# Loads one batch ahead, stores from the ScalarE queue, 128-partition q/k and two-bank PSUM tiles in a fused attention and gated FFN kernel

## The chip, the cores and the metric

The kernel runs on one core of a Trainium2 chip. The metric is the device time of one execution in microseconds (us); runs of one kernel in this study lie within some 1 to 3% of each other. A profile's span is about 1.7 us shorter than the time quoted for the same run. A run over 1.5% above the fastest of its kernel is counted as slow; only fast runs enter the ratios.

Engines: PE is TensorE, PEld its weight loads, DVE is VectorE, ACT is ScalarE, POOL is GpSimd, SP is SyncE, which here only issues transfers. The traces list each one's instructions in an order of their own, called its queue here (in the page of the kernel before, 2211 of PE and 269 of DVE).

## The reference, cut to what matters

```python
def _attn_ref(q, k, v):                 # (4, 8, 768, 64) each
    block, window = (32, 16)
    k_sum = k.reshape(B, H, nb, block, D).max(axis=3)     # 24 summary keys
    v_sum = v.reshape(B, H, nb, block, D).mean(axis=3)
    # scores on a band |i-j| < 16, and on the 24 summaries (+ log 32); one softmax
    # over both; the result times [v, v_sum]
def _moe_ref(x, w_gate, w_val, w_out):  # x: 3072 tokens x 512, d_ff 1536
    gate = 1 / (1 + exp(-(x @ w_gate)))
    return (gate * (x @ w_val)) @ w_out
```

## The kernel before

Queries go in 12 tiles of 64 per head; each tile sees 96 keys and 24 summaries. The kernel emits small units: T (transpose q and k of a head pair, build windows and summaries), S (scores and exp), V (sum v over blocks and spread the sums to all 12 tiles), A (attention times v), X (transpose the result into the FFN's input). Batch 0 goes through them alone, the head. After that the units of batch b+1 are strewn among the matmuls of the FFN of batch b. FFN of batch 3 runs alone.

```python
psum = ctx.enter_context(tc.tile_pool(name="psum", bufs=8, ...))   # one bank each, for all
...
def load_qk(b, p):       # 96 partitions of 8 tokens
    st = stg_pool.tile([128, 1024], FP32, ...)
    nc.sync.dma_start(out=st[0:96]..., in_=tap[b, 2*p:2*p+2].rearrange("h (p t) d -> p h (t d)", t=8))
...
def u_T(p):              # pk and pq are two tiles
    pk = ps([128, 8, 96], BF16, "pk")       # 8 transposes; VectorE copies and reduces it
    pq = ps([128, 8, 96], BF16, "pq")       # 8 transposes
    nc.scalar.copy(out=qT..., in_=view(pq, 0, [[1, 96], [96, 8]]))
...
def u_V():
    ...                  # 12 matmuls into vsp
    nc.vector.tensor_copy(out=vx[96:120, 0, :, 0:64], in_=vsp[96:120]...)
    nc.vector.tensor_copy(out=vx[96:120, 1:NQ, :, 0:64],
                          in_=vx[96:120, 0:1, :, 0:64].to_broadcast([NS, NQ - 1, H, 64]))
...
def u_2(hf, tt, part):   # second FFN layer; when a tile is done:
    nc.scalar.mul(out=ot, in_=m3, mul=0.5)
    nc.sync.dma_start(out=out[r:r + 128, :], in_=ot)      # same queue as the loads
...
for b in range(B):       # loads and casts of batch b+1 are emitted here, at the start of FFN b
```

The softmax here doesn't subtract the row's maximum and nothing guards it: scores larger than these inputs give would overflow.

## Time and profile before

313.96 us (313.77 to 314.0, 3 runs). To compare kernels I cut each profile at the second gate activation (the head and the first two FFN units are done) and at the last output tile of each batch. The lines that carry the reading stand in the prediction, whose own cuts lie up to 1.5 us earlier.

| us | head | FFN 0 + att. 1 | FFN 1 + att. 2 | FFN 2 + att. 3 | FFN 3 | end | span |
|---|---|---|---|---|---|---|---|
| before | 48.3 | 71.7 | 70.9 | 71.6 | 46.7 | 3.1 | 312.3 |

FFN 3 shows what a batch's FFN costs when nothing disturbs it. The other stages are some 25 us longer, and attention of a batch is 11.2 us of pure TensorE work: the rest is waiting, half clock (groups of four matmuls that take about 1.3 us instead of 0.65, at a granted clock of 0.50 from 76 to 81 us) and switching.

### The profile page before, as it was taken

The numbers are of one execution on the slowest core, as the hardware profiler recorded it, in microseconds if no ns is written. First come the engines' busy times: TensorE is split into PE (matmuls) and PEld (weight loads), VectorE is DVE, ScalarE is ACT, GpSimd is POOL, SyncE is SP. The second block draws the span as 40 slices with busy tenths as digits, with TensorE's granted clock in tenths as the row PEclk, the third lists the DMA queues.
The fourth block names the chain that finished last, engine by engine and source line by source line (L and its number), as shares of the span: only waits on it lengthen the run. The fifth ranks groups of instructions, "written<-read, shape, count | busy, mean of one in ns | idle before, by whom it ended". The sixth has DMA issues, their size and how long they took to land.

```text
span 312.3 us, 5516 instructions
## 1 busy us (share of the span) xinstructions
PE 261.3 (84%) x2211; PEld 145.6 (47%) x2224; DVE 159.1 (51%) x269; ACT 115.3 (37%) x221; POOL 83.6 (27%) x112
## 2 busy tenths in 40 slices
PE   1384669993995996899799997798799999999995
PEld 0332536661542543564455443563365545666542
DVE  5545944469836642685775311684676311444200
ACT  2640623341530553263165322362164333333221
POOL 8475863049700000675000000675000000000000
PEclk9999859997897999599999999799799999999999
DMA  7999999619600115995000025995000112000022
GB/s 216 263 214 320 385 292 252 239 41 241 151 36 0 60 43 176 280 197 115 0 3 2 34 93 182 262 212 121 2 0 2 37 67 101 2 0 3 0 101 101
DMA packets 54713, 37.84 MB, mean 121 GB/s; under 512 B 37792, under 2 KB 43936, under 8 KB 54688
## 3 DMA queue, kind: packets, MB, share of 16 engines
q1 hardware_dynamic: 54688, 37.49, 44.0%
q8 instruction: 17, 0.28, 0.4%
q14 instruction: 8, 0.07, 0.1%
HBM read 31.20 MB, written 6.29 MB: 120 GB/s over the span
## 4 chain that ended last, share of the span: by engine, by line
PE 62%; DMA 16%; DVE 12%; POOL 4%; SPq 3%; issue 1%; ACT 1%; POOLq 0%; ACTq 0%; DVEq 0%
PE m L326 21%; PE gp L309 17%; PE vp L309 16%; DMA qst<-in_q_dram 8%; DMA vst<-in_v_dram 7%; DVE vx L251 4%; PE av L262 3%; POOL vx L149 3%; SPq L109 2%; DVE kTx L204 2%; DVE xs L270 2%; PE br L283 2%; PE vsp L243 1%; PE sc L224 1%; DVE P L233 1%
## 5 line engine op out<-in xcount | busy, mean ns | idle before, releaser
L315 DVE SCALAR_TENSOR_TENSOR hT<-gate,vp 128x384 bf16<-128x384 f32 x96 | 52.8, 552 | 73.2 <-PE vp L309 73.0
L309 PE MATMUL gp<-xT,wg 128*128 128x384 bf16 x384 | 83.1, 341 | 0.0
L309 PE MATMUL vp<-xT,wv 128*128 128x384 bf16 x384 | 81.7, 337 | 0.0
L314 ACT ACTIVATE gate<-gp 128x384 f32<-128x384 f32 x96 | 47.2, 492 | 67.5 <-DVE hT L315 34.1
L326 PE MATMUL m<-wo,hT 128*128 128x512 bf16 x275 | 66.3, 384 | 0.8 <-issue 0.2
L309 PEld LDWEIGHTS <-wv 128*128 128x128 bf16 x384 | 38.7, 101 | 27.4 <-issue 4.0
L309 PEld LDWEIGHTS <-wg 128*128 128x128 bf16 x384 | 35.5, 101 | 24.0 <-issue 4.2
L124 POOL CAST qkbf<-kst 96x1024 bf16<-96x1024 f32 x12 | 12.8, 1067 | 108.9 <-DMA kst<-in_k_dram 90.4
L326 PEld LDWEIGHTS <-hT 128*128 128x128 bf16 x288 | 26.8, 98 | 29.7 <-issue 0.8
L230 ACT ACTIVATE P<-sc 128x384 bf16<-128x384 f32 x64 | 27.4, 499 | 16.4 <-PE sc L224 16.4
L211 ACT COPY qT<-pq 128x768 bf16<-128x768 bf16 x16 | 12.8, 798 | 49.8 <-PE pq L209 49.8
L331 ACT ACTIVATE ot<-m 128x512 f32<-128x512 f32 x24 | 14.3, 597 | 42.3 <-PE m L326 38.6
L149 POOL CAST vx<-vst 96x512 bf16<-96x512 f32 x40 | 24.6, 637 | 8.0 <-DMA vst<-in_v_dram 7.5
L233 DVE TENSOR_TENSOR P<-P,mask 128x768 bf16<-128x768 bf16 x32 | 21.7, 686 | 9.1 <-ACT P L230 9.0
L194 DVE COPY kTx<-pk 128x960 bf16<-128x960 bf16 x16 | 18.4, 1153 | 13.6 <-PE pk L191 13.6
L191 PE MATMUL pk<-ident,qkbf 96*128 96x96 bf16 x128 | 10.4, 239 | 16.8 <-ACT qkbf L120 9.9
L262 PE MATMUL av<-vx,P 120*64 120x65 bf16 x384 | 13.4, 210 | 11.9 <-DVE vx L251 10.3
L262 PEld LDWEIGHTS <-P 120*64 120x64 bf16 x384 | 9.9, 121 | 22.7 <-issue 21.2
L124 POOL CAST qkbf<-qst 96x1024 bf16<-96x1024 f32 x16 | 17.0, 1064 | 8.7 <-DMA qst<-in_q_dram 8.2
L270 DVE TENSOR_TENSOR xs<-av,rec 128x384 bf16<-128x384 f32 x32 | 17.8, 558 | 1.1
L286 ACT COPY xT<-br 128x768 bf16<-128x768 bf16 x16 | 12.8, 800 | 15.0 <-PE br L283 14.9
L243 PE MATMUL vsp<-vx,zsum 96*32 96x512 bf16 x48 | 15.3, 437 | 3.6 <-POOL vx L149 3.4
(39 smaller groups left out, 159.8 us busy)
## 6 DMA issues: line engine op xcount, KB each, us to landing
vst<-in_v_dram SPq DMA_DIRECT2D x40, 192.0 KB, 3.7
kst<-in_k_dram SPq DMA_DIRECT2D x16, 384.0 KB, 8.0
qst<-in_q_dram SPq DMA_DIRECT2D x16, 384.0 KB, 9.0
out_dram<-ot SPq DMA_DIRECT2D x24, 256.0 KB, 2.0
wst<-in_moe_w_gate_dram SPq DMA_DIRECT2D x6, 512.0 KB, 7.8
wst<-in_moe_w_val_dram SPq DMA_DIRECT2D x6, 512.0 KB, 7.9
wst<-in_moe_w_out_dram SPq DMA_DIRECT2D x6, 512.0 KB, 11.5
vedge<-in_v_dram SPq DMA_DIRECT2D x8, 160.0 KB, 4.8
```

Source lines behind the costliest of these rows:

```text
L124: nc.gpsimd.tensor_copy(out=bf, in_=src)
L149: nc.gpsimd.tensor_copy(out=dst, in_=st)
L194: nc.vector.tensor_copy(out=kTx[:, 1:11, 0:W].rearrange("p t (a w) -> p t a w", w=8), in_=view(pk, 6, [[8, 10], [1, 12], [96, 8]]))
L230: nc.scalar.activation(out=P[:, i, 6 * hf:6 * hf + 6, :].rearrange("p t w -> p (t w)"), in_=sc[i], func=ACT.Exp, scale=SCALE)
L233: nc.vector.tensor_tensor(out=P[:, :, 6 * hf:6 * hf + 6, :].rearrange("p i t w -> p i (t w)"), in0=P[:, :, 6 * hf:6 * hf + 6, :].rearrange ...
L243: nc.tensor.matmul(out=vsp[96:128].rearrange("p (h d) -> p h d", h=H), lhsT=zsum[:, 30 - 2 * t:62 - 2 * t], rhs=vx[0:W, t, :, 0:64], start ...
L262: nc.tensor.matmul(out=av[r:r + 64, t6 // 2, i, 0:65], lhsT=P[0:KX, i, t, :], rhs=vx[0:KX, t, 2 * p + i, 0:65], start=True, stop=True)
L270: nc.vector.tensor_tensor(out=xs.rearrange("p a i d -> p (a i) d"), in0=av[:, :, :, 0:64].rearrange("p a i d -> p (a i) d"), in1=rec.rearr ...
L309: nc.tensor.matmul(out=o, lhsT=wb[:, c, 128 * f:128 * (f + 1)], rhs=xT[:, c, HALF * hf:HALF * (hf + 1)], start=(c == 0), stop=(c == NP - 1))
L314: nc.scalar.activation(out=gate, in_=gp, func=ACT.Tanh, scale=0.5)
L315: nc.vector.scalar_tensor_tensor(out=hT[hf][:, f, :], in0=gate, scalar=1.0, in1=vp, op0=ALU.add, op1=ALU.mult)
L326: nc.tensor.matmul(out=m3, lhsT=hT[hf][:, f, 128 * tt:128 * (tt + 1)], rhs=wo_bf[:, f], start=(f == 0), stop=(f == NF - 1))
```

## The change

Its intent: the SyncE queue should never stand behind an output tile, so stores move to ScalarE's queue and loads are emitted a batch earlier; transfers should use all partitions; attention should need fewer evictions; the head should start on less data. The core of the diff, cut (`# ...` marks cuts):

```diff
-psum = ctx.enter_context(tc.tile_pool(name="psum", bufs=8, ...))
+psum = ctx.enter_context(tc.tile_pool(name="psum", bufs=4, ...))     # FFN, vsp, br of b>0
+psum2 = ctx.enter_context(tc.tile_pool(name="psum2", bufs=2, ...))   # two banks each: attention
 # ...
-    in_=tap[b, 2 * p:2 * p + 2].rearrange("h (p t) d -> p h (t d)", t=8)
+    in_=tap[b, 2 * p:2 * p + 2].rearrange("h (p t) d -> p h (t d)", t=6)
 # ...
+        def T(self, p):
+            at = psum2.tile([128, 2, 1024], BF16, name="tp", tag="at")
+            pk = at[:, 0, 0:S]...          # one tile holds both
+            pq = at[:, 1, 0:S]...
 # ... V:
+            copy("dve" if self.b == 0 else "act", vx[96:120, 0, :, 0:64], vsp[96:120]...)
+            if self.b == 0:                # by head pair: two on VectorE, two on POOL
+                for p in range(NP):
+                    copy("dve" if p < 2 else "pool", vx[96:120, 1:NQ, 2*p:2*p+2, 0:64], ...)
+            else:
+                nc.scalar.dma_start(out=vx[96:120, 1:NQ]..., in_=vx[96:120, 0:1]...to_broadcast(...))
 # ... X:
+            if self.b == 0:
+                br = psum2.tile([128, 2, 1024], BF16, name="br2", tag="at")[:, 0, 0:S]
 # ... second FFN layer:
-                nc.sync.dma_start(out=out[r:r + 128, :], in_=ot)
+                nc.scalar.dma_start(out=out[r:r + 128, :], in_=ot)
 # ... order of the head: T0 T1, casts of v, S0 S1, loads of the rest, V, then
+    for u in att[0].units("A0 T2 A1 X0 S2a S2b X1 T3 A2 S3a S3b X2"):
 # ... FFN b:
-                s_ = load_qk(nb, p)
+                load_cast_qk(b + 2, p)
+    HEAD = "T0 T1 S0a S0b T2 S1a S1b"
+    TAIL = "V A0 S2a S2b T3 X0 A1 S3a S3b X1 A2 X2 A3 X3"
```

## The prediction

> **What bounds the kernel now.** I read the page first: which engine is fullest, and in which slices it is not full.
>
> ```profile
> PE 261.3 (84%) x2211; PEld 145.6 (47%) x2224; DVE 159.1 (51%) x269; ACT 115.3 (37%) x221; POOL 83.6 (27%) x112
> ...
> PE   1384669993995996899799997798799999999995
> ...
> POOL 8475863049700000675000000675000000000000
> PEclk9999859997897999599999999799799999999999
> DMA  7999999619600115995000025995000112000022
> ```
>
> TensorE is the bound, but not everywhere. Slices are 7.8 us each. It is thin in the first six (the head, up to 44 us, where batch 0 goes through attention alone), and has dents near 70 us, near 125 us and near 200 us, where the granted clock dips as well. The second and third dents lie where POOL and DMA wake up after long zeros: the loads of the next batch arrive late. The waits of TensorE over the span and those of the SyncE queue say why (us in total, times, longest):
>
> ```profile
> PE av L262 <- DVE vx L251: 10.3, 4, 2.9
> PE pk L191 <- ACT qkbf L120: 9.9, 3, 5.5
> PE pk L191 <- POOL qkbf L124: 6.9, 2, 3.8
> PE br L283 <- DVE xs L270: 5.6, 7, 2.0
> PE sc L224 <- DVE kTx L204: 5.4, 1, 5.4
> ...
> SPq L333 <- ACT ot L331: 161.3, 23, 34.7
> ```
>
> The last line is the load problem: the output stores stand in the same in-order queue as the loads, and that queue sat 161.3 us waiting for finished output tiles. The 6.9 us in two waits of pk are its price, once each in batch 1's and batch 2's FFN. The 5.4 us wait is a third thing, read from the timeline (start, length, engine, line):
>
> ```profile
> 69.44 6.61 DVE L204 COPY kTx<-kTx 128x264 bf16<-128x264 bf16 x1
> ...
> 71.00 5.96 POOL L176 CAST wo<-wst 128x1024 bf16<-128x1024 f32 x6
> ...
> 76.12 0.45 PE L224 MATMUL sc<-qT,kTx 64*128 64x64 bf16 x10 [5.43 <-DVE kTx L204]
> ```
>
> That copy's median over 16 instances is 234 ns. Here it took 6.61 us while POOL ran ten casts end to end.
>
> From the chain of waits, the stages are: head and first FFN units to about 46.8 us; FFN of batch 0 with attention of batch 1 to 120.5 (73.7); FFN 1 with attention 2 to 191 (70.5); FFN 2 with attention 3 to 262 (71); FFN 3 alone to 308.5 (46.5); last stores 3.8. The 313.96 us quoted is 1.7 above the 312.3 us span.
>
> [...] 238 GB/s in the first 15 us (96-partition q/k, DMA share 0.94) against 353 GB/s from 25 to 44 us, where mostly 128-partition weights move. [...] after the 5.4 us wait a group of four matmuls took 1.40 and 1.28 us, where the warm one takes 0.65. [...]the 256 KB output stores land 2.0 us after issue.
>
> **The change, part by part.**
>
> Pure work first, from warm stretches. An FFN unit is 0.65 + 0.65 us, so 24 are 31.2; 72 second-layer matmuls at 0.217 are 15.6; FFN per batch 46.8 us. Attention per head pair: T 0.68 (16 transposes of 96 columns), S 0.56, A 0.56, X 0.34; per batch 4 x 2.14 + 2.6 (V, 12 x 0.217) = 11.2. So 58 us per full stage; the 70.5 us of FFN 1 hold 12.5 us of waste: 7.0 of listed waits (pk 3.8, av 2.3, pq 0.4, vsp 0.5), about 2.3 of half clock after the late load, about 2.2 in some twenty groups that take 0.76 instead of 0.65 after a switch, and 1 unexplained.
>
> q/k in 128 partitions of 6: T becomes 12 transposes of 128 columns; 1536 columns both ways, so 0 on TensorE. Casts shrink from 1024 to 768 elements (1.05 to about 0.8 us). On VectorE the 1.15 + 0.31 us strided PSUM copies become one 768-element PSUM copy (estimate 0.95, by scaling) and a plain SBUF copy of the windows [...]. [...]
>
> Two-bank PSUM tiles: one Exp of 768 for two of 499 ns, one xs for two of 558, one reciprocal for two of 191. [...] In exchange FFN has four banks instead of a share of eight: two units in flight. Where VectorE runs T0 and T1 (2.5 us each) between hT operations, I estimate 1 us of TensorE stall per stage.
>
> Loads ahead, stores on ScalarE: takes the pk/pq/vsp waits and their cold restarts out of FFN 1 and FFN 2: 4.7 + 2.3 = 7 us each. Stores put about 24 issues on an engine 37% busy: hidden.
>
> V spread: VectorE's 3.08 us broadcast becomes, for batches 1 to 3, a ScalarE copy (0.7) and an SBUF to SBUF transfer of 24 x 11 rows of 1056 bytes = 279 KB, at least the 2.0 us of a store [...]. V end to A0 is then about 5 us against 4.0 now. In FFN 1 and 2 one unit (1.3) stands between, so the wait grows from 2.3 to about 3.5; in FFN 0 A0 follows V directly, so about 5 against 3.7, and the clock goes cold (1 to 1.5).
>
> Head: q/k of two pairs (1.57 MB) load first, over two queues, then v (2.3 MB), then the rest. At some 300 and 215 to 240 GB/s, v is in at about 17.5 us and V ends near 18.7 instead of 25.96. Its spread takes 0.7 + 0.8 us for the first pair instead of 3.8. But T2 has moved behind V, so the VectorE chain after V holds two T, four masks, four A: about 15 us of work [...]. I put X3 at 39.7 and the first FFN units (three quarters done early) at 40.4, against 46.8 now: 6.4 gained.
>
> Sum: head 40.4. FFN 0: 44.2 + 11.2 = 55.4 pure, + 2.2 switches + 5 V + 1.5 cold [...] + 1 X = 68. FFN 1 and 2: 58 + 2.2 + 3.5 + 1 cold + 1 stall = 65.5 each. FFN 3: 46.6. End 3.8 + 1.7. Total 291.5; I round down to **290 us** as the unexplained parts were counted as staying.
>
> **The rivals.** (a) The V transfer replaces the load wait: if it takes 5 us or more and the clock goes cold each time, FFN 0 to 2 lose 3 us each more: 299. [...] Against: 279 KB is about the size of a 2.0 us store. (b) [...] POOL now streams casts through all of FFN 0[...]. One more event like the 6.6 us one costs some 8 us with the clock: 298. Against: in the new order POOL follows the DMA (1.45 us per 512 KB at 353 GB/s against a 1.04 us cast)[...]. (c) Four FFN banks starve TensorE: 2 us more per stage, 296. (d) Better than planned: the head's VectorE chain overlaps well (X3 at 36) and the clock stays up: 281. (e) The loads were hidden anyway, no gain: contradicted by 6.9 us of pk waits and the late wake-up of POOL.
>
> **Range and chances.** Two of (a), (b), (c) together give about 305, all good gives 280. Range 280 to 300. To miss 2% (307.7) more than two rivals must hit: faster 0.93, same 0.05, slower 0.02.
>
> **What would show it.** Right: no pk wait on POOL after 60 us; SyncE queue free of waits on ot; first full FFN units at 38 to 42 us; FFN 1 and 2 at 64 to 67 us; q/k loads over 300 GB/s; av's wait on a DMA of 3 to 5 us in place of vx L251. Wrong: av waits over 5 us, a VectorE copy of several us beside POOL, gp or vp waiting for hT, or a head that still ends near 46 us.

What no trace of this case shows is cut out of the prediction, and each cut is marked. A term of the sum is among the cuts, 3 us of stalls in FFN 0: with it the terms of FFN 0 come to 68, and the whole to 291.5. The 5 and 3.5 us for V rest on 3.5 us for the transfer, and v's arrival on 300 GB/s for q/k; both were estimates (measured in r0_after: 4.2 to 4.4 us from issue to the reader, and 353 to 401 GB/s). "Cold" and "half clock" stand for what the kernel before shows after the 5.4 us wait, a granted clock of 0.50 from 76 to 81 us. Measured there too: the 768-element PSUM copy takes 0.96 us and the window copy 0.54, 1.50 together for 1.46 before; the 32 Exps of 768 keep ScalarE busy for 25.6 us, where 64 of 384 took 27.4; and a set of six transposes of 128 columns takes 0.34 us at full speed, as eight of 96 did.

## The result, and the profile after

The changed kernel took 297.07 us median (296.26 to 299.95, 4 runs; one of them counted as slow) against 313.98 us (4 runs by then). The ratio of the fast runs is 0.942, interval 0.9357 to 0.9483. Every ratio here is the mean time of one kernel's fast runs over that of the kernel before in the same rounds, so it is not quite the ratio of the medians quoted. A difference of two ratios is turned into us with the 315 us of before.

The readings below are of a second run of the same kernel, r0_after. First its page: span, busy time, then some rows of 40 slices, 7.4 us each.

```profile
span 296.1 us, 5337 instructions
...
PE 256.3 (87%) x2160; PEld 143.3 (48%) x2160; DVE 136.8 (46%) x236; ACT 115.3 (39%) x192; POOL 81.3 (27%) x116
...
PE   1384587999985999898799999996999999999995
...
POOL 8749467776710553220036100000000000000000
PEclk9996557999995999999799999999799999999999
DMA  7995999999926299900108121001000111000022
```

POOL and DMA now have their work early: the casts of the last batch are over by slice 23, and the dents of TensorE that came with late loads are gone. Three dents remain (slices 13, 20 and 28; the granted clock dips in 13, 20 and 29), and the head is thin as before (all of its first seven slices are below 9). What TensorE waits for:

```profile
PE av L268 <- DMA vx<-vx: 10.7, 3, 4.1
PE tp L195 <- ACT qkbf L114: 8.6, 2, 5.9
PE tp L197 <- POOL qkbf L118: 3.8, 2, 2.6
PE sc L226 <- DVE kTx L208: 2.2, 1, 2.2
PE sc L226 <- ACT qT L205: 1.4, 1, 1.4
PE gp L323 <- ACT gate L330: 1.3, 3, 0.8
...
PE br L291 <- ACT qT L205: 1.1, 1, 1.1
PE sc L226 <- ACT xT L294: 0.9, 1, 0.9
```

The first line is the new wait: A0 on V's transfer, once in each of three stages, and the three dents. Nothing waits for POOL's casts after the head. By stages:

| us | head | FFN 0 | FFN 1 | FFN 2 | FFN 3 | end | span |
|---|---|---|---|---|---|---|---|
| before | 48.3 | 71.7 | 70.9 | 71.6 | 46.7 | 3.1 | 312.3 |
| r0_after | 49.1 | 65.9 | 66.1 | 65.4 | 46.7 | 2.9 | 296.1 |

The three mixed stages gave 16.8 us. The head, reordered from end to end, gave nothing: it is 0.8 us longer, which is within its scatter (below).

### The profile page after: what moved, and what is told of

Read it like the earlier page. It is cut to its first block, busy times and chain, and to the rows that moved or that the text cites. A ratio compares the mean times of both kernels' runs of the same rounds, so it can differ in the third digit from the quotient of the medians.

```text
span 298.2 us, 5324 instructions
## 1 busy us (share of the span) xinstructions
PE 257.9 (86%) x2147; PEld 144.1 (48%) x2160; DVE 137.3 (46%) x236; ACT 115.2 (39%) x192; POOL 81.8 (27%) x116
## 4 chain that ended last, share of the span: by engine, by line
PE 76%; DVE 10%; DMA 4%; POOL 3%; ACT 3%; issue 2%; POOLq 0%
PE m L340 21%; PE vp L323 20%; PE gp L323 20%; PE vsp L243 4%; DMA vx<-vx 4%; DVE kTn L201 3%; PE sc L226 3%; PE av L268 2%; DVE kTx L208 2%; PE br L291 2%; PE tp L197 2%; DVE kTx L207 2%; PE tp L195 2%; DVE xs L277 1%; DVE hT L331 1%
## 5 line engine op out<-in xcount | busy, mean ns | idle before, releaser
L330 ACT ACTIVATE gate<-gp 128x384 f32<-128x384 f32 x96 | 46.7, 493 | 56.7 <-DVE hT L331 31.9
L118 POOL CAST qkbf<-qkst 128x768 bf16<-128x768 f32 x28 | 23.0, 838 | 58.8 <-issue 31.1
L232 ACT ACTIVATE P<-sc 128x768 bf16<-128x768 f32 x32 | 25.6, 811 | 13.1 <-PE sc L226 12.1
L233 DVE TENSOR_TENSOR P<-P,mask 128x768 bf16<-128x768 bf16 x32 | 20.6, 651 | 15.5 <-ACT P L232 15.4
L205 ACT COPY qT<-tp 128x768 bf16<-128x768 bf16 x16 | 12.8, 798 | 36.8 <-DVE kTn L201 36.8
L268 PE MATMUL av<-vx,P 120*64 120x65 bf16 x384 | 11.5, 211 | 12.5 <-DMA vx<-vx 10.7
L201 DVE COPY kTn<-tp 128x768 bf16<-128x768 bf16 x16 | 15.3, 955 | 11.2 <-PE tp L197 10.8
L275 DVE RECIPROCAL rec<-av 128x12 f32<-128x12 f32 x16 | 3.7, 228 | 36.4 <-PE av L268 36.4
L226 PE MATMUL sc<-qT,kTx 64*128 64x64 bf16 x384 | 12.9, 204 | 5.3 <-DVE kTx L208 2.0
L195 PE MATMUL tp<-ident,qkbf 128*128 128x128 bf16 x96 | 9.2, 241 | 8.5 <-ACT qkbf L114 8.5
L226 PEld LDWEIGHTS <-kTx 64*128 64x128 bf16 x384 | 8.7, 102 | 15.8 <-issue 10.4
```

Source lines behind the costliest of these rows:

```text
L118: nc.gpsimd.tensor_copy(out=out, in_=in_)
L195: nc.tensor.transpose(pk[:, t, :], kb[:, t].rearrange("p h d -> p (h d)"), ident)
L201: nc.vector.tensor_copy(out=kTn[:, 16:16 + S].rearrange("p (a t) -> p a t", t=6), in_=pk.rearrange("p t a -> p a t"))
L226: nc.tensor.matmul(out=sc[:, i, QT * t6:QT * (t6 + 1)], lhsT=kTx[64 * i:64 * i + 64, t, :], rhs=qT[64 * i:64 * i + 64, QT * t:QT * (t + 1) ...
L232: nc.scalar.activation(out=Ph, in_=sc[:, :, 0:6 * QT], func=ACT.Exp, scale=SCALE)
L233: nc.vector.tensor_tensor(out=Ph, in0=Ph, in1=mask[:, None, 6 * hf:6 * hf + 6, :].rearrange("p i t w -> p i (t w)") .to_broadcast([128, 2, ...
```

## The experiments

Every kernel here gave a correct result. The theory after the first look: the loads' part works; the head's gain is lost in waits that the change itself adds (a PSUM tile shared by q and k, only two attention buffers, POOL's part of V's spread); and V's transfer is a loss.

### The head: r0_after, a1_br_mm, a2_pq_own, a3_q_dve

> The changed kernel once more, for a profile in the fast state and its spread. Expected 294 to 298 us, ratio to before 0.94. In the fast profile the first FFN units again end near 50 us (46.8 before), and the three stages after it take about 65, 67 and 65 us.

Measured: 297.76 us (297.54 to 297.82), ratio 0.9443 (0.9406 to 0.948). This ratio is the base for all that follows.

How far the head of a single profile can be trusted: b1, b2, c1 and c3 below leave the head as it is in r0_after, and theirs took 47.6, 48.0, 48.4 and 48.4 us against 49.1. So a difference of 1.5 us between two heads can be scatter. The granted clock does not explain it: in slices 4 and 5 of the pages (about 22 to 36 us) it is 0.9 or more in b1 and c1, 0.6 and then 0.5 in r0_after, and 0.7 and then 0.5 in b2.

The chain of waits of r0_after through the start of the head (start us, length us, engine, what):

```profile
7.01 0.83 POOL qkbf L118
...
7.89 0.83 PE tp L197 x6
...
8.75 0.97 DVE kTn L201
...
9.75 0.80 ACT qT L205
10.55 0.74 ACT qkbf L114
...
11.33 0.82 PE tp L195 x6
```

k of pair 0 had been transposed by 6.8 us, but VectorE's copy of it (kTn) starts at 8.75, when q's transposes in the same tile are done; and the instruction stream has ScalarE's copy of q (qT) wait for kTn, though it reads the other bank. Behind qT in ScalarE's queue stands the cast of pair 1's k. In r0_after qT waited for kTn all 16 times.

a1: X of batch 0 takes one-bank tiles of the FFN pool for pairs 0 to 2.

```diff
-            if self.b == 0:
+            if self.b == 0 and p == 3:
                 br = psum2.tile([128, 2, 1024], BF16, name="br2", tag="at")[:, 0, 0:S]
```

> Batch 0's transposed outputs (X of pairs 0 to 2) take a one-bank PSUM tile of the FFN pool instead of one of the two two-bank tiles. Theory (two two-bank buffers serialise batch 0's attention after V): the waits of br on qT (1.1 us), of sc on xT (0.9) and of br on P (0.3) go, head 1.5 to 3 us shorter. Rival (VectorE's own chain is the bound there): under 0.5 us.

Measured: 295.52 us, ratio 0.9353 (0.9293 to 0.9414), some 2.8 us less than r0_after, though the two intervals just overlap; the head is 46.1 us, below all five above. The waits of br on qT (1.1 us) and on P (0.3) are gone; that of sc on xT, which the theory also named, is not (0.9 to 1.3 us), so that step of it missed. All of TensorE's waits in the head fell only from 22.9 to 22.5 us; its busy time fell from 26.0 to 23.4, as the same matmuls ran faster. So the two attention buffers were a ring that br waited on for 1.4 us; that the ring cost the whole gain is not shown.

a2: batch 0's pq in a tile of its own.

```diff
-            pq = at[:, 1, 0:S].rearrange("p (t a) -> p t a", t=6)
+            pq = (ps([128, S], BF16, "pq") if self.b == 0 else at[:, 1, 0:S]).rearrange(...)
```

> Batch 0's pq in a tile of its own, so that the kTn copy waits for pk alone and qT does not wait for kTn. Theory (the shared tile couples q to k: q0's late cast delays kTn, kTn delays qT, qT delays k1's cast on ScalarE): first kTn at about 6.8 us instead of 8.76, V starts about 1.5 us earlier, head 2 to 3.5 us shorter. Rival (v's arrival and the cold V set the head): under 0.7 us.

Measured: 294.36 us, ratio 0.9331 (0.9271 to 0.9392), some 3.5 us less; head 45.3 us. The timeline of a2 (start, length, engine, line, operation):

```profile
7.02 0.96 DVE L201 COPY kTn<-tp 128x768 bf16<-128x768 bf16 x1 [5.38 <-PE tp L195]
...
9.45 0.83 ACT L114 CAST qkbf<-qkst 128x768 bf16<-128x768 f32 x1
...
14.94 4.93 PE L243 MATMUL vsp<-vx,zsum 96*32 96x512 bf16 x12
```

kTn waits for pk's transposes alone and starts 1.7 us earlier; k's cast follows 1.0 us earlier (10.44 in the timeline of r0_after), V 1.6 us (16.52 in r0_after). The coupling by the shared tile is shown.

a3: q of pairs 0 and 1 cast on VectorE (`cast_qk(st0[p][1], "dve")` for `"pool"`), so that it does not wait for POOL's set-up.

> q of pairs 0 and 1 cast on VectorE, which is idle there, instead of behind POOL's set-up (which ends at 7.02 us). Theory (POOL's set-up starts the head's chain): pq of pair 0 at about 6.7 instead of 7.9 us, V's start 1 to 2 us earlier, head 1 to 2 us shorter. Rival (V waits for v's casts, last at 19.4 us): under 0.5 us.

Measured: 297.63 us, ratio 0.9436 (0.9375 to 0.9497): no difference that can be told. In its profile V starts at 15.17 us and the head is 1.1 us shorter, which is within the scatter, and the time as a whole does not show it. POOL's set-up is at most a small part.

### The stages: b2_v_early, b1_v_dve, c1_stores_sp, c3_both_undone

b2: V of batches 1 to 3 earlier in the order of units.

```diff
-    HEAD = "T0 T1 S0a S0b T2 S1a S1b"
-    TAIL = "V A0 S2a S2b T3 X0 A1 S3a S3b X1 A2 X2 A3 X3"
+    HEAD = "T0 T1 S0a S0b T2 V S1a S1b"
+    TAIL = "A0 S2a S2b T3 X0 A1 S3a S3b X1 A2 X2 A3 X3"
```

> The changed kernel with V of batches 1 to 3 issued several units ahead of A0 (between T2 and S1a) instead of right before it. Theory (A0 waits for V's transfer, 4.1, 3.3 and 3.3 us, and each wait leaves TensorE at half clock for about 2 us more): the av wait on the transfer falls below 1 us in all, the three FFN stages get 4 to 7 us shorter each, 280 to 286 us. Rival (the wait only moves, to hT or to a PSUM bank): less than 5 us gained, 293 or more.

Measured: 281.98 us (280.14 to 284.22), ratio 0.8974 (0.8903 to 0.9045), about 15 us less than r0_after by the ratios (12.6 us in the three stages of the profiles); FFN 1 and 2 take 60.9 and 60.1 us instead of 66.1 and 65.4. What the wait had cost is seen in FFN 1 of r0_after:

```profile
138.28 0.83 ACTq L256 DMA_DIRECT2D vx<-vx  x1
...
142.50 0.54 PE L268 MATMUL av<-vx,P 120*64 120x65 bf16 x22 [3.28 <-DMA vx<-vx]
...
143.63 1.44 PE L323 MATMUL vp<-xT,wv 128*128 128x384 bf16 x4
144.87 1.49 PE L323 MATMUL gp<-xT,wg 128*128 128x384 bf16 x4
146.15 1.28 PE L323 MATMUL vp<-xT,wv 128*128 128x384 bf16 x4
```

The transfer takes 4.2 us from issue to the matmul that it releases, 3.28 of them waiting, and the groups of four that follow start 1.24 and 1.28 us after one another, where warm ones start 0.65 apart; with the next one that makes some 2 us more (the granted clock of slice 20, 140.6 to 148.1 us, is 0.7). One wait is left in b2, in FFN 0, so "below 1 us in all" missed:

```profile
79.38 1.42 ACTq L256 DMA_DIRECT2D vx<-vx  x1
...
89.40 0.54 PE L268 MATMUL av<-vx,P 120*64 120x65 bf16 x22 [4.41 <-DMA vx<-vx]
```

Here the same transfer takes 10.0 us. It was issued among batch 2's loads; that it queued behind them is likely, since the mean busy share of the DMA engines is 0.96 from 79 to 90 us, against 0.27 around the same transfer in r0_after (87 to 92.5 us), but no run takes those loads away.

b1: V's spread of batches 1 to 3 back on VectorE, as in the kernel before.

> V's spread of batches 1 to 3 back on VectorE (0.70 + 3.08 us), all else as changed. Theory (the transfer is the longer of the two): A0 waits about 1 us less in each stage, 294 to 297 us. Rival (3.8 us on VectorE starve the four FFN banks): waits of vp or gp on hT appear and it is over 299 us.

Measured: 292.43 us (291.91 to 293.35), ratio 0.9307 (0.9265 to 0.9348), 4.3 us less than r0_after, a little better than either theory. The same place in FFN 1:

```profile
135.00 3.08 DVE L116 COPY vx<-vx 24x5632 bf16<-24x5632 bf16 x1
...
138.13 0.82 PE L266 MATMUL av<-vx,P 120*64 120x65 bf16 x22 [2.32 <-DVE vx L116]
```

After this wait the next group of four is 1.46 us long in the trace, against 0.82 at 143.02 us; after a wait of 2.31 us in FFN 1 of the kernel before, the next was 0.82 at once (151.12 us). The copy that was replaced is 1.1 us faster than the transfer, and VectorE has room for it: vp waits for hT 0.7 us in all. This part of the change was a loss.

c1: only the stores go back to SyncE (`nc.sync.dma_start(out=out[r:r + 128, :], in_=ot)`), the loads stay ahead.

> Output stores back in the SyncE queue, loads still emitted one batch ahead. Theory (either half alone unblocks the loads): no pk/tp wait on POOL after 60 us, 296 to 300 us. Rival (the queue is what matters): waits of tp on POOL of 3 us in the stages of FFN 1 and FFN 2, 303 us or more.

Measured: 297.04 us, ratio 0.9443 (0.9395 to 0.949): the same as r0_after. A kernel with the other half alone undone (loads emitted late, stores on ScalarE) was built, not run: it has the same instructions in the same order on every engine as the changed kernel, because without stores in it the SyncE queue holds only loads.

c3: both undone: stores on SyncE, and batches 2 and 3 loaded in the loop as `load_cast_qk(b + 1, p)`, after the stores of the batch before.

> Output stores back in the SyncE queue and loads of batches 2 and 3 emitted only after the stores of the batch before, as in the kernel before. Theory (late loads cost 3 to 4 us of waiting and some 2 us of half clock in each of FFN 1 and FFN 2): waits of tp on POOL of 3 to 4 us twice, 306 to 311 us. Rival (loads were hidden in this version anyway): under 300 us.

Measured: 305.86 us (305.47 to 307.84), ratio 0.9748 (0.9689 to 0.9807), 9.6 us more than r0_after, and than c1, which ran in c3's rounds; it is just under the range expected. TensorE's waits of c3 that r0_after does not have:

```profile
PE tp L195 <- POOL qkbf L118: 6.1, 2, 3.1
```

Late loads are worth 9.6 us here, and either half of the repair is enough.

### Together: e1_combo, e2_combo_q, w1_warm, e3_combo_qv

e1 puts a1, a2 and b2 together and has VectorE spread batch 1's V (the first copy for `self.b <= 1`, and a second branch):

```diff
+            elif self.b == 1:
+                copy("dve", vx[96:120, 1:NQ, :, 0:64],
+                     vx[96:120, 0:1, :, 0:64].to_broadcast([NS, NQ - 1, H, 64]))
```

> Together: V issued early, batch 1's V spread by VectorE (its transfer had waited 10 us among the loads of batch 2 when V came early), batch 0's X of pairs 0 to 2 and batch 0's pq in one-bank tiles. Theory (the parts are independent: 15 from V early, about 3.5 from pq, 1 to 2 from br, 4 to 6 from batch 1's V): 270 to 276 us, no wait of av on a transfer, first FFN units at about 43 to 45 us. Rival (the head's two edits repair one and the same wait, and VectorE's 3.8 us in FFN 0 come back as waits on hT): 278 us or more.

Measured: 275.79 us (275.36 to 276.58), ratio 0.8779 (0.8689 to 0.8869). The stages are 44.4, 58.9, 61.2, 60.1 and 46.8 us, and no unit waits for a transfer of V. The head's two edits seem to overlap: 4.7 us together, 3.0 and 3.8 alone, with a scatter of 1.5.

e2: as e1, and the casts of pairs 2 and 3 of batch 0 are emitted ahead of `att[0].V()`, so POOL does them before its share of V's spread.

> As e1, with the casts of q of pairs 2 and 3 issued ahead of POOL's part of V's spread (pq of pair 2 waited 2.6 us for POOL). Theory (that wait is on the head's path): that wait falls below 1 us and the head is 1 to 2.5 us shorter than e1's. Rival (VectorE's work after V sets the head): under 0.5 us.

Measured: 277.66 us, ratio 0.8821 (0.8697 to 0.8945), within e1's spread and not below it. The head is 1.1 us shorter (43.3 us), as the theory said but within the scatter; the wait of pq on POOL fell from 3.8 us (2.6 the longer) to 1.0. FFN 0 is 2.9 us longer. In its list of waits stands a new one, of vsp:

```profile
PE vsp L243 <- POOL vx L118: 2.1, 4, 0.7
...
PE pq L197 <- POOL qkbf L118: 1.0, 1, 1.0
```

Batch 1's V came before batch 1's v had landed.

w1: e2 with needless matmuls (`nc.tensor.matmul(out=d[:, 0:128], lhsT=ident, rhs=ident, ...)`) in the head's gaps, meant to keep TensorE at full speed.

> As e2, with 66 needless matmuls in the head's gaps (34 before the first transposes, 12 and 8 after T0 and T1, 12 after V), which write a tile nobody reads. Theory (half clock in the head costs time: V takes 4.9 us there and 2.7 later, a set of six transposes 0.65 and 0.34): V takes about 3 us and the head is 1 to 3 us shorter than e2's. Rival (V then waits for v's casts, and VectorE sets the rest): under 0.7 us, or slower by the added matmuls.

Measured: 276.74 us, ratio 0.8806 (0.8716 to 0.8896), not to be told from e2. The first eight of V's matmuls took 1.90 us, 0.24 each as in a later batch (2.76 for twelve), but V ended at 21.3 us, later than e2's 20.2, since it now waits for the casts of v. The head is 45.0 us. The casts themselves were late in this profile, the last ending at 20.69 us (19.02 in e2), so the run does not say what full speed gains when v is on time; in e2 V ended 1.2 us after the last cast, which bounds what V's end could gain. Faster matmuls were worth nothing there while data was late.

e3: e2 with batch 1's V one place later, `"T0 T1 S0a S0b T2 S1a V S1b"`.

> As e2, with batch 1's V one place later in FFN 0 (after S1a). In e2 the shorter head was lost again: batch 1's V waited 2.1 us in four pieces for casts of v that had not landed. Theory (v of batch 1 arrives at a time that the head's length does not change): vsp's wait on POOL falls below 1 us and the ratio to before is 0.87 to 0.88, at or just below e1's 0.878. Rival (something else cost e2 its head gain): the ratio stays at e2's 0.882 or above with vsp's wait gone.

Measured: 274.77 us (273.11 to 275.51, 6 runs), ratio 0.8756 (0.8702 to 0.8811): the lowest, though its interval overlaps e1's. vsp no longer waits for POOL, FFN 0 is 59.0 us with the head at 43.4. Its page:

```profile
span 273.6 us, 5335 instructions
...
PE 249.7 (91%) x2160; PEld 140.5 (51%) x2160; DVE 140.3 (51%) x238; ACT 113.6 (42%) x191; POOL 80.4 (29%) x116
...
PE   1496668999999999899999999999999999999994
...
PEclk9999777999999999999999999999999999999999
```

After the seventh slice TensorE is 90% busy or more (but for slice 17, 80 to 90%, and the last one) and the granted clock does not dip. What is left is the head. e3 beats both kernels, by 12.4% and some 7%.

All profiles by stage:

| us | head | FFN 0 | FFN 1 | FFN 2 | FFN 3 | end | span | ratio |
|---|---|---|---|---|---|---|---|---|
| a1_br_mm | 46.1 | 64.6 | 66.2 | 65.3 | 46.8 | 2.9 | 291.9 | 0.9353 |
| a2_pq_own | 45.3 | 65.2 | 66.1 | 65.2 | 46.8 | 2.9 | 291.5 | 0.9331 |
| a3_q_dve | 48.0 | 66.5 | 66.0 | 65.3 | 46.8 | 2.9 | 295.5 | 0.9436 |
| b1_v_dve | 47.6 | 64.4 | 64.5 | 64.3 | 46.7 | 3.2 | 290.7 | 0.9307 |
| b2_v_early | 48.0 | 63.8 | 60.9 | 60.1 | 46.8 | 2.9 | 282.5 | 0.8974 |
| c1_stores_sp | 48.4 | 65.6 | 65.8 | 65.2 | 46.8 | 2.9 | 294.7 | 0.9443 |
| c3_both_undone | 48.4 | 67.4 | 68.5 | 70.1 | 46.8 | 2.9 | 304.1 | 0.9748 |
| e1_combo | 44.4 | 58.9 | 61.2 | 60.1 | 46.8 | 3.0 | 274.4 | 0.8779 |
| e2_combo_q | 43.3 | 61.8 | 61.4 | 60.1 | 46.8 | 2.9 | 276.3 | 0.8821 |
| w1_warm | 45.0 | 59.2 | 61.0 | 60.1 | 46.7 | 3.0 | 275.0 | 0.8806 |
| e3_combo_qv | 43.4 | 59.0 | 61.3 | 60.2 | 46.7 | 3.0 | 273.6 | 0.8756 |

## Why the prediction was right or wrong

It named 290 us, and 297.07 was measured, inside its range of 280 to 300 and faster by over 2%, as forecast. The 7 us are almost all one term, the head; that the other stages came out close is in part errors that cancel.

**The head: wrong.** "I put X3 at 39.7 and the first FFN units at 40.4, against 46.8 now: 6.4 gained." X3's copy ended at 47.7 us and the head at 49.1 (48.3 before). From the timeline of r0_after, V and X3's copy:

```profile
16.52 4.86 PE L243 MATMUL vsp<-vx,zsum 96*32 96x512 bf16 x12
...
46.91 0.80 ACT L294 COPY xT<-br 128x768 bf16<-128x768 bf16 x1 [5.93 <-PE br L291]
```

Two terms of it were too small. V was to end near 18.7 and ended at 21.4. v had landed as planned (its last packets at 17.7 us, 17.5 planned), but POOL's last cast of it ended only at 19.26; V's start waited for T1, held up by the shared tile (a2 moved start and end by 1.6 and 1.5 us), and its matmuls ran at little over half speed, 4.86 us for the twelve against 2.76 in a later batch (the granted clock on the page does not dip there, 0.9 or more in slice 3). The time from V's end to X3 was to be 21.0 us and was 26.3 (24.5 in b1 and b2, which have the same head). The prediction saw the limit there as "the VectorE chain after V", about 15 us of work; the runs point to three other waits: q coupled to k (a2, shown), the ring of two attention buffers (a1, 1.4 us of it shown), and q's cast behind POOL's share of V's spread (e2, a wait of 2.6 us gone and the time within scatter). With all three repaired, in e2, V's end to X3 takes 21.4 us (20.2 to 41.6), near the 21.0 predicted. So the estimate of the work was about right, and the waits that the new tiles and order bring with them were missing from it; how the time divides among the three, and how much of it is slow matmuls, stays open. The prediction counted the two-bank tiles as a matter of evictions and of FFN banks, never of attention's own buffers.

**Loads and stores: right in kind, too large.** "7 us each" for FFN 1 and 2. c3 against r0_after gives 9.6 us for both, 2.4 in FFN 1 and 4.7 in FFN 2 by the profiles; FFN 0 is 1.5 us longer too, with no wait that says why. The wait came back as 3.1 us twice, as expected; the half clock after it cost less than the 2.3 us that I had read in the kernel before. The two halves are also not a sum: c1 shows that the loads ahead are enough.

**V's spread: right in the wait, too small in the clock.** Predicted waits were about 5, 3.5 and 3.5 us; they were 4.8 (0.7 for ScalarE's copy, 4.1 for the transfer), 3.3 and 3.3. Of the clock I wrote "1 to 1.5" and "1 cold". b2 takes two waits and their half clock away, for 5.2 and 5.3 us in FFN 1 and 2, so the clock's part is nearer 2. Rival (a) named the right culprit at a smaller size. The recorded 65.5 for FFN 1 and 2 (its terms add up to 65.7) agrees with 66.1 and 65.4 partly by luck: the clock cost 1 us more, and the 1 us of stalls did not come.

**The four FFN banks and the long copy: right that they would not rule, and put too high.** The sum held 3, 1 and 1 us of stalls for them. Rival (c) put up to 2 us per stage on the banks; gp's wait on gate is 1.3 us and vp's on hT 0.2 us over the whole span of r0_after. Rival (b) did not come: the longest window copy on VectorE took 1.10 us (median 0.54), the summary copy 0.85 at most, where the kernel before had one of 6.61. The "ten casts" beside that copy ran from 67.05 to 76.96 us; eight of them overlap it, and no run shows that they held it up. FFN 0 took 5.8 us less than before; the prediction's 73.7 to 68 is 5.7, again with the stalls too high and V's clock too low.

**The sum of pure work: right.** 58 us per mixed stage plus 2.2 of switches is 60.2; FFN 2 of b2, e1 and e3 takes 60.1 to 60.2. FFN 3 stayed at 46.7.

**q/k loads over 300 GB/s: right.** In r0_after v's packets (256 bytes) start at 5.9 us, so from 3 to 6 us only q and k move: 353, 395 and 401 GB/s in the three microseconds, against 318, 262 and 270 before. From 8 to 16 us v comes in alone, still in 96 partitions, at 213 to 215, so that the first 15 us together move 230 GB/s against 238 before. The recorded 238, used there as the rate of 96-partition q/k, averages in two microseconds in which almost nothing moved. Packet size (1536 bytes for 2048) and the second queue for q changed with the partitions; pairs 2 and 3, all from SyncE, also reached 352 (18 to 19 us). What the 128 partitions alone are worth stays open.

## What to carry to other kernels

When two values are put in one PSUM tile to save evictions, check which instruction now waits for which: readers on two engines become coupled (in r0_after qT waited for kTn all 16 times), and a pool of fewer, larger tiles can become a ring that engines wait on (br, for 1.4 us of the head). A transfer that replaces a copy must be issued early enough to land before its reader; moving it a few units ahead was worth 13 to 15 us here, nearly as much as the whole change (17). After shortening one stage, look at once for the next piece of data that is now too late: in e2 FFN 0 lost 2.9 us when batch 1's V came before its v had landed, and moving one unit by one place got it back.
